# Heads 27 to 31 laid out so that neighbours in the ring come with one load

## The chip, the cores and the metric

The kernel runs on one core of a Trainium2 chip. A time is the device time in microseconds (us) of one execution of the whole program. The kernel before was run three times; its time is the median of these runs. All data is float32.

## The reference

Two layers, each an attention block against a cached K and V and a ReLU MLP, are applied twice over with the same weights and the same cache, to one token x of width 640:

```python
def _A_ref(x, k_cache, v_cache, wq, wo):          # 32 heads, 8192 keys, head width 128
    q = (x @ wq).reshape(1, 1, 32, 128).transpose(0, 2, 1, 3)
    scores = einsum("bhqd,bhkd->bhqk", q, k_cache) * (128 ** -0.5)
    p = softmax(scores, axis=-1)
    o = einsum("bhqk,bhkd->bhqd", p, v_cache)
    return o.transpose(0, 2, 1, 3).reshape(1, 1, 4096) @ wo

def _B_ref(x, w1, w2):                            # 640 -> 1728 -> 640
    return maximum(x @ w1, 0) @ w2

x = x + _A_ref(_layernorm(x), k_cache, v_cache, wq, wo)
x = x + _B_ref(_layernorm(x), w1, w2)
x = x + _A_ref(_layernorm(x), k_cache, v_cache, wq, wo)
x = x + _B_ref(_layernorm(x), w1, w2)
```

K and V of all heads are 256 MiB together, and both layers need all of it.

## The kernel before, in words

**The ring.** K and V come from DRAM into one SBUF tile, `ring`, of 8 x 4760 elements on each of 128 partitions. Places in it are counted in units of 8 elements. One head is 2048 units (16384 elements, 64 KiB on each partition): four K pieces and four V pieces of 256 units each. The whole ring thus holds a little more than two heads. Layer 0 goes through the heads 0 to 31, layer 1 through 31 to 0, so that what is in the ring at the change of layers can be used again: parts of heads 29 and 30 and all of 31, 3960 units (`KEPT`), stay there. The rest of the ring at that time (800 units) takes the blocks of w2, in four loads.

**Units of loading.** `UNITS` (L42) gives for each head the units in which it lies in DRAM. Heads 0 to 26 are one unit each, K and V together; `PARTS` (L44) says at which pieces the load of such a unit is cut. Heads 27 to 31 are cut into several units: 27 into K and V, 28 into four halves, 29 into ten units, 30 into five and 31 into six. `DROPPED` (L64) says from which unit on a head of 29 or 30 is kept for layer 1. Each unit is its own contiguous block in DRAM, with one row for each partition. The DRAM array is filled by `_laid_out` (L1006) on the host, in the order of `UNITS`.

**The order of the loads.** `todo` is a list of loads for the whole program, in order. An entry is a unit, the first and last piece, and a place in the ring or none. `pump` (L207) takes entries from its front as long as there is room: for an entry without a place `place` (L181) looks for a free stretch of the ring, and for the kept units of heads 29 and 30 `apart` (L123) gives the stretch to look in. If the entry at the front finds no room, `pump` stops; entries behind it don't overtake. `release` (L239) is called where the program has recorded the last matmul that reads a piece; it marks the piece's place free and calls `pump`. So each load stands on SyncE's queue behind the release that made room for it, and waits there for that matmul. A few loads go through ScalarE's queue instead: wq and wo of four heads at a time (tile `pair`), w1 and a rest of w2.

**The work of one head.** `scores` (L480) multiplies one K piece with the query, in eight matmul records, on TensorE; `row_maxima` and `exponentials` make the softmax with VectorE and ScalarE; `values` (L528) multiplies one V piece with the weights, again eight records; `output` (L562) sums four groups of rows. On TensorE the order is: scores of a head, softmax, values, output, scores of the next head. Only for the first three heads of layer 1 (`AHEAD`) do the next head's scores begin earlier. The lines that the profile names are L485 (scores), L534 and L552 (values), L456 (products with wo and w2), L667 (first MLP product) and L390 (`keep_busy`: matmuls without use that keep TensorE active, among them one in the softmax of the third last and of the second last head of a layer, and two between the second and third value piece of the second last head of layer 1).

**The end of a layer.** The second last head (30 in layer 0, 1 in layer 1) is projected through wo before the last head is done. `before_last` (L726) makes the layer norm and most of the first MLP product from that, between the scores of the last head (31, or 0). When the last head's values are there, a product with `mix` adds its share to the MLP, the hidden row is transposed, and the w2 blocks are multiplied, block by block. In layer 0 the release of the first two w2 blocks makes room for the fourth w2 load. After it SyncE loads units 0 and 1 of head 30 into two tiles that are no longer needed (`wct` and `mix`, `load_beside`, L227), and after that the first units of head 29 for layer 1, as the w2 blocks are done.

In layer 0 the loads from head 27 on stand in the order of heads and units: 27 K, 27 V, 28 in four, 29 in ten, 30 in five, 31 in six, w2 in four. In layer 1 they are: 29 in nine (the tenth is kept), 28 in four, 27 in two, 26 in two, and so on down to head 1 in four loads (`PARTS[1, 1]` = [2, 4, 6, 8], two pieces each), head 0 in six and w2 in four.

Of the kernel before, what the change touches and what calls it, by code (L numbers as in the profile page):

```python
# [43 lines left out]
PARTS = {(0, 0): [4, 9], (1, 26): [4, 8], (1, 25): [4, 8], (1, 2): [4, 8], (1, 1): [2, 4, 6, 8], (1, 0): [2, 4, 6, 7, 8, 9]}  # L44
# [19 lines left out]
DROPPED = {29: 9, 30: 2}  # L64
KEPT = 3960
# [40 lines left out]
def decode_kernel(ctx: ExitStack, tc: tile.TileContext, x, kv, wqo, w1, w2, w2_rest, out):  # L106
# [16 lines left out]
    apart = {(29, 9): (3800, KEPT), (30, 0): (4464, 4544), (30, 1): (4544, RING), (30, 2): (3072, 3800)}  # L123
# [3 lines left out]
    def all_of(layer, u):  # L127
        todo.append((layer, u, 0, len(UNITS[u[0]][u[1]][1]), None))
# [8 lines left out]
    def turning(layer, heads, slot):  # L137

        for h in heads:
            for a, end in parts_of(layer, h):  # L140
                while a < end:
                    b = min(end, a + SLOTS - slot)
                    todo.append((layer, (h, 0), a, b, SLOT * slot))
                    slot = (slot + b - a) % SLOTS
                    a = b

    def anywhere(layer, h):
        for a, b in parts_of(layer, h):
            todo.append((layer, (h, 0), a, b, None))
# [4 lines left out]
    for h in range(FULL[-1] + 1, H):  # L154
        for i in range(len(UNITS[h])):
            all_of(0, (h, i))
    for u in W2_ALL:
        all_of(0, u)
    for h in range(H)[:FULL[-1]:-1]:
        if h != 30:  # L160
            for i in range(len(UNITS[h])):
                if (h, i) not in kept:
                    all_of(1, (h, i))
# [5 lines left out]
    for u in W2_ALL:  # L169
        all_of(1, u)  # L170
    source = {}
    for us, dram in ((order, kv), (W2_ALL, w2)):
        o = 0
        for u in us:
            n = 8 * P * size(UNITS[u[0]][u[1]])
            source[u] = dram[o : o + n].rearrange("(p m) -> p m", p=P)
            o += n
# [29 lines left out]
    def pump():  # L207
        while todo:
            layer, u, first, last, at = todo[0]
            unit = UNITS[u[0]][u[1]]  # L210
            ns = [wide(kind_of(unit, t), piece) for t, piece in enumerate(unit[1])]
            n = sum(ns[first:last])
            if at is None:
                at = place(layer, u, n)
# [5 lines left out]
            o = 8 * sum(ns[:first])  # L220
            nc.sync.dma_start(ring[:, 8 * at : 8 * (at + n)], source[u][:, o : o + 8 * n])
            for t in range(first, last):
                live[layer, u, t] = at, ns[t]
                at_of[layer, u, t] = ring, 8 * at
                at += ns[t]

    def load_beside(where, at, n):  # L227
# [3 lines left out]
        nc.sync.dma_start(where[:, at : at + n], source[u])  # L231
# [774 lines left out]
def _laid_out(A_x, A_k_cache, A_v_cache, A_wq, A_wo, B_w1, B_w2):  # L1006
# [5 lines left out]
    for h in range(H):  # L1012
# [57 lines left out]
```

## Time and profile before

| | |
|---|---|
| median of 3 runs | 1349.7 us (1349.62 to 1351.87) |
| span of the profiled execution, first to last instruction | 1347.3 us |
| mean granted TensorE clock | 0.812 |
| TensorE busy with matmuls | 801.4 us |
| VectorE busy | 251.6 us |
| bytes moved by DMA | 574.55 MB, 426 GB/s over the span |
| share of SyncE's queue in the time of the 16 DMA engines | 91.7% |
| share of ScalarE's queue | 7.7% |
| loads | 157 |

The profiled execution is one of its own and not one of the three timed runs; what is known of its time is the span, which is 2.4 us below the median of the runs.

How to read it: a page of the profile gives busy time by engine, then the span in 40 slices, the DMA queues, the chain of work that ended last, the costliest groups of instructions and the DMA issues by size. Beside it the trace answers queries. A row of the timeline has start, duration, engine, line of the kernel, operation, output and inputs, shape and count; in square brackets stands how long the engine was idle before it and what ended that. A row of the chain has start, duration and what was done; for a DMA the duration is from its issue to its landing. A row of the windows has for one stretch of time each engine's busy time and number of instructions, then the granted TensorE clock (1 is full speed), the DMA engines' busy share and GB/s. A DMA share a little over 1 comes from packets that overlap.

### The profile page before, as it was taken

The page shows a single profiled execution, that of the slowest core. Times are in us where ns is not written, and L with a number is a line of the kernel's source. Part 1 is how long each engine was busy: PE and PEld are TensorE (multiplying, and loading weights), DVE is VectorE, ACT ScalarE, POOL GpSimd, SP SyncE. Part 2 cuts the span into 40 slices and gives each one's busy share as a digit, 9 for nine tenths or more (in the row PEclk, how much of TensorE's full clock was granted, in tenths as well). Part 3 has the DMA queues.
Part 4 walks back from the last instruction along what each step waited for, and adds up shares of the span by engine and source line. Part 5 has one row for each costly group of instructions (what it writes and reads, how often), then busy time and mean ns, then how long its engine had stood idle before and what let it go on. Part 6 is the DMA issues. An engine that isn't in the chain of part 4 may idle for free.

```text
span 1347.3 us, 13949 instructions
## 1 busy us (share of the span) xinstructions
PE 801.4 (59%) x6258; PEld 274.7 (20%) x6258; DVE 251.6 (19%) x798; ACT 58.5 (4%) x149; POOL 2.9 (0%) x10
## 2 busy tenths in 40 slices
PE   3455565563655655467688554456466554647777
PEld 1111111121211211122253111112122111212224
DVE  1121111221212211121223211122111121111222
ACT  0000000000000000000000000000000000000000
POOL 0000000000000000000000000000000000000000
PEclk9687677887978967787799877798778788877789
DMA  9999999999999999999999999999999999999997
GB/s 409 433 427 435 432 439 426 442 412 435 438 431 430 428 435 425 442 424 405 425 397 425 434 431 440 421 446 424 438 430 427 428 438 438 435 413 442 425 423 331
DMA packets 22675, 574.55 MB, mean 426 GB/s; under 512 B 2516, under 2 KB 2648, under 8 KB 5464
## 3 DMA queue, kind: packets, MB, share of 16 engines
q1 hardware_dynamic: 19592, 529.84, 91.7%
q10 hardware_dynamic: 3024, 43.83, 7.7%
q8 instruction: 49, 0.80, 0.2%
q14 instruction: 10, 0.08, 0.0%
HBM read 573.65 MB, written 0.00 MB: 426 GB/s over the span
## 4 chain that ended last, share of the span: by engine, by line
DMA 62%; PE 28%; DVE 6%; ACT 1%; issue 1%; another core or an unknown queue 1%; SPq 0%; ACTq 0%; DVEq 0%
DMA ring<-in_kv 61%; PE ps L485 14%; PE outs L534 9%; DVE h_t L496 2%; ACT p L510 1%; DMA pair<-in_wqo 1%; DVE pt L514 1%; PE pm L501 1%; DVE p L571 1%; PE px L424 1%; PE px L456 1%; PE acc L456 1%; DVE pT L516 0%; PE px L652 0%
## 5 line engine op out<-in xcount | busy, mean ns | idle before, releaser
L485 PE MATMUL ps<-ring,spread_q 128*32 128x512 f32 (+3 forms) x2104 | 328.4, 775 | 309.0 <-DMA ring<-in_kv 304.1
L534 PE MATMUL outs<-ring,pT 128*4 128x512 f32 (+1 forms) x2032 | 265.0, 665 | 41.5 <-DMA ring<-in_kv 24.7
L485 PEld LDWEIGHTS ps<-ring,spread_q 128*32 128x32 f32 x2104 | 77.6, 138 | 496.3 <-issue 296.9
L496 DVE TENSOR_REDUCE h_t<-ps 128x1 f32<-128x512 f32 x64 | 44.3, 692 | 612.5 <-PE ps L485 612.5
L510 ACT ACTIVATE p<-ps,h_t 128x512 f32<-128x512 f32 x64 | 44.0, 687 | 1225.5 <-DVE h_t L508 1225.5
L534 PEld LDWEIGHTS outs<-ring,pT 128*4 128x4 f32 x2032 | 51.2, 93 | 194.7 <-issue 169.9
L581 PE MATMUL pm<-ones,p 128*128 128x1 f32 x120 | 23.0, 260 | 94.9 <-DVE p L571 94.9
L567 DVE TENSOR_SCALAR p<-outs,ind 128x128 f32<-128x128 f32 x60 | 21.1, 351 | 262.1 <-PE outs L534 262.1
L571 DVE SCALAR_TENSOR_TENSOR p<-outs,ind,p 128x128 f32<-128x128 f32 x180 | 63.1, 351 | 6.4
L514 DVE STREAM_TRANSPOSE pt<-p 128x512 f32<-128x512 f32 x64 | 46.5, 727 | 58.5 <-ACT p L510 58.5
L501 PE MATMUL pm<-row_of,h_t 128*128 128x16 f32 x128 | 25.5, 274 | 49.9 <-DVE h_t L496 49.0
L581 PEld LDWEIGHTS pm<-ones,p 128*128 128x128 f32 x120 | 17.8, 188 | 151.7 <-DVE p L571 150.4
L501 PEld LDWEIGHTS pm<-row_of,h_t 128*128 128x128 f32 x128 | 19.2, 189 | 109.3 <-DVE h_t L496 107.4
L424 PE MATMUL px<-pair,ln_xc 128*32 128x256 f32 x280 | 34.6, 395 | 4.4 <-ACT mix L660 4.4
L652 PE MATMUL px<-w_t,wct 128*128 128x448 f32 (+1 forms) x80 | 35.1, 553 | 1.1 <-ACT wct L645 1.1
L523 PE MATMUL pm<-ind,h_t 128*128 128x1 f32 x128 | 23.6, 253 | 18.3 <-ACT p L510 18.3
L523 PEld LDWEIGHTS pm<-ind,h_t 128*128 128x128 f32 x128 | 22.1, 202 | 36.2 <-ACT p L510 27.2
L456 PE MATMUL acc<-pair,o_cols 128*32 128x160 f32 x496 | 21.6, 313 | 0.6 <-DVE o_cols L606 0.6
L424 PEld LDWEIGHTS px<-pair,ln_xc 128*32 128x32 f32 x280 | 15.6, 112 | 21.2 <-ACT mix L660 8.5
L582 DVE TENSOR_SCALAR o_cols<-pm,h_t 128x1 f32<-128x1 f32 x60 | 13.1, 218 | 30.3 <-PE pm L581 30.3
L508 DVE TENSOR_REDUCE h_t<-pm 128x1 f32<-128x16 f32 x64 | 11.2, 175 | 32.2 <-PE pm L501 32.2
L456 PEld LDWEIGHTS acc<-pair,o_cols 128*32 128x32 f32 x496 | 15.2, 113 | 3.9 <-issue 1.8
(119 smaller groups left out, 217.8 us busy)
## 6 DMA issues: line engine op xcount, KB each, us to landing
ring<-in_kv SPq DMA_DIRECT2D x24, 4096.0 KB, 30.5
ring<-in_kv SPq DMA_DIRECT2D x11, 6144.0 KB, 34.7
ring<-in_kv SPq DMA_DIRECT2D x31, 2048.0 KB, 31.1
pair<-in_wqo ACTq DMA_DIRECT2D x13, 2560.0 KB, 25.9
ring<-in_kv SPq DMA_DIRECT2D x14, 1024.0 KB, 12.7
ring<-in_w SPq DMA_DIRECT2D x4, 1280.0 KB, 25.8
w_t<-in_w ACTq DMA_DIRECT2D x1, 4320.0 KB, 27.7
pair<-in_wqo ACTq DMA_DIRECT2D x3, 1280.0 KB, 13.7
```

What stands on the lines that cost most here:

```text
L424: nc.tensor.matmul(pq[32 * j : 32 * j + 32, :n], xc[:, c : c + 1].to_broadcast([P, 32]), wq_t[g][:, c, j * n : (j + 1) * n], start=(c == 0 ...
L456: nc.tensor.matmul(acc[32 * g : 32 * g + 32, :DR], col.to_broadcast([col.shape[0], 32]), wt[:, g * DR : (g + 1) * DR], start=first, stop=last,
L485: nc.tensor.matmul(hd.ps[32 * g : 32 * g + 32, c : c + n], spread_q[:, 3 - r : 35 - r], tile_of[:, at + g * n : at + (g + 1) * n], start=f ...
L496: nc.vector.tensor_reduce(hd.nm, hd.ps, AX.X, ALU.max, negate=True)
L501: nc.tensor.matmul(pt[:, :16], hd.nm.to_broadcast([P, P]), row_of.rearrange("p g r -> p (g r)"), start=True, stop=True,)
L510: nc.scalar.activation(hd.p, hd.ps, AF.Exp, bias=hd.low, scale=1.0, accum_out=hd.l)
L514: nc.vector.transpose(pt, hd.p)
L523: nc.tensor.matmul(pt[:, :1], hd.l.to_broadcast([P, P]), ind[:, 4:5], start=True, stop=True)
L534: nc.tensor.matmul(hd.out[32 * g : 32 * g + 4, r : r + m].rearrange("p r d -> p (r d)"), hd.pT[:, 4 * i : 4 * i + 4], tile_of[:, v : v + m ...
L571: nc.vector.scalar_tensor_tensor(oc[:, r], hd.out[:, r], ind[:, r : r + 1], oc[:, r - 1], op0=ALU.mult, op1=ALU.add,)
L581: nc.tensor.matmul(pt[:, :1], oc[:, 3], ones, start=True, stop=True)
L652: nc.tensor.matmul(pt[:, :n], wct[:, c], w1_t[:, c, f : f + n], start=(c == 0), stop=(c == NB - 1),)
```

## The change

The loads around the change of layers are written out by hand. `ROWS` says which units lie side by side in DRAM: each of the heads 0 to 28 is a row, the units of heads 29 and 30 together are one row in a new order, and head 31 is a row. `ENDS` lists the loads from head 27 on in layer 0, `STARTS` the first loads of layer 1 down to head 27. One load can now take several units that are neighbours in the row and in the ring. The kept units of 30 and 29 come earlier in layer 0: unit 2 of head 30 with unit 9 of head 29 between the K and the V of head 28, and units 0 and 1 of head 30 after that V, ahead of head 29's other units. In `PARTS` head 1 of layer 1 has two loads of four pieces and no longer four of two. `pump` and `_laid_out` follow. In layer 0 there are 12 loads fewer, in layer 1 six.

```diff
-PARTS = {(0, 0): [4, 9], (1, 26): [4, 8], (1, 25): [4, 8], (1, 2): [4, 8], (1, 1): [2, 4, 6, 8], (1, 0): [2, 4, 6, 7, 8, 9]}
+PARTS = {(0, 0): [4, 9], (1, 26): [4, 8], (1, 25): [4, 8], (1, 2): [4, 8], (1, 1): [4, 8], (1, 0): [2, 4, 6, 7, 8, 9]}
...
+ROWS = [[(h, i) for i in range(len(UNITS[h]))] for h in range(29)]
+ROWS.append([(29, i) for i in (0, 1, 2, 3, 6, 4, 5, 7, 8)] + [(30, 2), (29, 9), (30, 0), (30, 1), (30, 3), (30, 4)])
+ROWS.append([(31, i) for i in range(len(UNITS[31]))])
+ENDS = [
+    [(27, 0), (27, 1)],
+    [(28, 0), (28, 1)],
+    [(30, 2), (29, 9)],
+    [(28, 2), (28, 3)],
+    [(30, 0), (30, 1)],
+    ROWS[29][:5],
+    ROWS[29][5:9],
+    [(30, 3)],
+    [(30, 4)],
+] + [[u] for u in ROWS[30]]
+STARTS = [
+    [(29, 0)],
+    [(29, 1)],
+    [(29, 2)],
+    [(29, 3)],
+    ROWS[29][4:8],
+    [(29, 8)],
+    [(28, 0), (28, 1)],
+    [(28, 2)],
+    [(28, 3)],
+    [(27, 0)],
+    [(27, 1)],
+]
...
-    apart = {(29, 9): (3800, KEPT), (30, 0): (4464, 4544), (30, 1): (4544, RING), (30, 2): (3072, 3800)}
+    apart = {(30, 2): (3072, KEPT), (30, 0): (4464, RING)}
...
-    for h in range(FULL[-1] + 1, H):
-        for i in range(len(UNITS[h])):
-            all_of(0, (h, i))
-    for u in W2_ALL:
-        all_of(0, u)
-    for h in range(H)[:FULL[-1]:-1]:
-        if h != 30:
-            for i in range(len(UNITS[h])):
-                if (h, i) not in kept:
-                    all_of(1, (h, i))
+    for us in ENDS + [[u] for u in W2_ALL]:
+        all_of(0, us)
+    for us in STARTS:
+        all_of(1, us)
...
-            nc.sync.dma_start(ring[:, 8 * at : 8 * (at + n)], source[u][:, o : o + 8 * n])
-            for t in range(first, last):
-                live[layer, u, t] = at, ns[t]
+            u, t = pieces[0]
+            block, o = source[u]
+            unit = UNITS[u[0]][u[1]]
+            o += 8 * sum(wide(kind_of(unit, i), unit[1][i]) for i in range(t))
+            nc.sync.dma_start(ring[:, 8 * at : 8 * (at + n)], block[:, o : o + 8 * n])
+            for (u, t), m in zip(pieces, ns):
+                live[layer, u, t] = at, m
                 at_of[layer, u, t] = ring, 8 * at
-                at += ns[t]
+                at += m
```

The orders of TensorE, VectorE, ScalarE and GpSimd are the same instructions in the same order before and after; only the line numbers differ (L520 and L569 take the places of L485 and L534). What moves stands on SyncE's queue. The numbers in its rows are partitions and elements on each partition; 4096 elements are a 2048 KB load.

On SyncE in layer 0, from the last of the undivided heads to the loads of head 30, before: the rows are two undivided loads, the second of them head 26 (16384), then 27 (8192), 28 (4096), 29 (from 2048 to 1280), the kept units 0 and 1 of 30 (640, 1728), and behind these rows 30's unit 2 (5824), its V and head 31.

```order
L221 DMA ring<-in_kv 128x16384 x2
L221 DMA ring<-in_kv 128x8192 x2
L221 DMA ring<-in_kv 128x4096 x4
L221 DMA ring<-in_kv 128x2048 x2
L221 DMA ring<-in_kv 128x1024
L221 DMA ring<-in_kv 128x1280
L221 DMA ring<-in_kv 128x2048 x2
L221 DMA ring<-in_kv 128x512
L221 DMA ring<-in_kv 128x2048 x2
L221 DMA ring<-in_kv 128x1280
L221 DMA ring<-in_kv 128x640
L221 DMA ring<-in_kv 128x1728
```

And the same place after: the third 16384 is head 27, 8192 is head 28's K, 7104 the kept units 2 of head 30 and 9 of head 29, 8192 head 28's V, 2368 the kept units 0 and 1 of head 30, 6912 head 29's K and 8192 its V.

```order
L255 DMA ring<-in_kv 128x16384 x3
L255 DMA ring<-in_kv 128x8192
L255 DMA ring<-in_kv 128x7104
L255 DMA ring<-in_kv 128x8192
L255 DMA ring<-in_kv 128x2368
L255 DMA ring<-in_kv 128x6912
L255 DMA ring<-in_kv 128x8192
L255 DMA ring<-in_kv 128x4096 x5
```

The kept units moved from behind head 29 to ahead of it, so that between head 29's V and the K halves of head 31 (the third and fourth of the five 4096 rows) only two loads are left.

On SyncE at the end of layer 1, before: heads 3 and 2 (8192), then head 1 in four loads and the first three of head 0 (4096), and the rest of head 0.

```order
L221 DMA ring<-in_kv 128x8192 x4
L221 DMA ring<-in_kv 128x4096 x7
L221 DMA ring<-in_kv 128x2048
L221 DMA ring<-in_kv 128x1024 x2
L221 DMA ring<-in_w 128x2560 x2
```

And after, where head 1 stands among the 8192 rows:

```order
L255 DMA ring<-in_kv 128x8192 x6
L255 DMA ring<-in_kv 128x4096 x3
L255 DMA ring<-in_kv 128x2048
L255 DMA ring<-in_kv 128x1024 x2
L255 DMA ring<-in_w 128x2560 x2
```

Four loads of 4096 became two of 8192: head 1's K and its V each land as a whole.

59 lines of the change are left out of this document (35 added, 24 removed).

## The prediction

> **What bounds the kernel now.** First the page of the profile, its head, its second and its third part.
>
> ```profile
> span 1347.3 us, 13949 instructions
> ...
> PE 801.4 (59%) x6258; PEld 274.7 (20%) x6258; DVE 251.6 (19%) x798; ACT 58.5 (4%) x149; POOL 2.9 (0%) x10
> ...
> DMA  9999999999999999999999999999999999999997
> ...
> DMA packets 22675, 574.55 MB, mean 426 GB/s; under 512 B 2516, under 2 KB 2648, under 8 KB 5464
> ```
>
> The DMA engines are busy in every fortieth of the span but the last. So whatever moves the time either makes the stream of loads shorter, stops it, or acts after its last load. The table of DMA issues says how far ahead the stream is issued: half of the 2048 KB loads land 31.1 us or more after their issue.
>
> ```profile
> ring<-in_kv SPq DMA_DIRECT2D x11, 6144.0 KB, 34.7
> ring<-in_kv SPq DMA_DIRECT2D x31, 2048.0 KB, 31.1
> ```
>
> Next the windows: two stretches with large rows and with rows of 8 KB, and three around the change of layers (time, then PE, PEld, DVE, ACT, POOL; the last three numbers are the granted clock, the DMA share and GB/s).
>
> ```profile
> 646.00:650.00 4.00, 0.51 (x20) 0.24 (x12) 0.00 (x0) 0.00 (x0) 0.00 (x0) 0.92 1.01 416
> 820.00:860.00 40.00, 20.16 (x170) 6.09 (x170) 5.55 (x17) 1.56 (x4) 0.00 (x0) 0.79 1.00 432
> 630.00:640.00 10.00, 7.13 (x48) 1.73 (x40) 2.15 (x7) 0.78 (x2) 0.00 (x0) 0.83 0.93 372
> 690.00:700.00 10.00, 9.18 (x196) 6.79 (x184) 2.59 (x14) 0.61 (x3) 0.00 (x0) 1.00 0.93 366
> 700.00:710.00 10.00, 8.63 (x132) 5.07 (x126) 2.19 (x13) 0.00 (x0) 1.10 (x2) 1.00 1.00 396
> ```
>
> There is little to win: 16 GB/s where rows are small, 1.4 us of stream at 630 to 640 ((432 - 372) x 10 / 432), and 2.4 us at 690 to 710 (66 and 36 GB/s below 432, for 10 us each).
>
> Last the chain that ended last, around the change of layers and at the end.
>
> ```profile
> 658.73 22.56 DMA ring<-in_kv
> ...
> 681.34 1.97 PE ps L485 x16
> ...
> 1294.64 28.89 DMA ring<-in_kv
> ...
> 1323.57 1.97 PE ps L485 x16
> ...
> 1342.90 1.27 PE px L456 x32
> ```
>
> And from SyncE's timeline the issue of the last w2 load of layer 0, and of the first eight ring loads of layer 1.
>
> ```profile
> 696.78 0.33 SPq L221 DMA_DIRECT2D ring<-in_w  x1
> ...
> 699.75 11.31 SPq L221 DMA_DIRECT2D ring<-in_kv  x8
> ```
>
> In both layers the second K half of the last head lands (658.73 + 22.56 = 681.29; 1294.64 + 28.89 = 1323.53), TensorE scores it at once, and from there the chain is compute only: in layer 0 to the release that lets SyncE issue the last w2 load at 696.78, which restarts a stream that had run dry, and in layer 1 to the end. The stream and TensorE therefore meet at two points. A gain of the stream counts only if TensorE is ready there, and lateness of TensorE counts in full, because the ring is full of kept heads and nothing else can be loaded.
>
> **How ready TensorE is.** The timeline of TensorE before the first point: the last scores of head 29 (its last K piece), its values, scores of 30, its values, first K piece of 31, the last MLP step, second K half of 31.
>
> ```profile
> 651.91 1.29 PE L485 MATMUL ps<-ring,spread_q 128*32 128x320 f32 x8 [5.40 <-DMA ring<-in_kv]
> ...
> 656.78 4.99 PE L534 MATMUL outs<-ring,pT 128*4 128x512 f32 x32
> ...
> 664.46 3.49 PE L485 MATMUL ps<-ring,spread_q 128*32 128x80 f32 x40
> ...
> 671.31 3.62 PE L534 MATMUL outs<-ring,pT 128*4 128x512 f32 x32 [0.64 <-DVE pT L516]
> ...
> 677.20 1.04 PE L485 MATMUL ps<-ring,spread_q 128*32 128x512 f32 x8
> ...
> 680.29 0.50 PE L667 MATMUL px<-w_t,ln_xc 128*32 128x192 f32 x8
> ...
> 681.34 1.93 PE L485 MATMUL ps<-ring,spread_q 128*32 128x512 f32 x16 [0.56 <-DMA ring<-in_kv]
> ```
>
> TensorE has 0.56 us to spare. And before the second point, in layer 1: scores of head 1, its four value pieces with fillers (L390) between the pairs, the projection, the two K halves of head 0.
>
> ```profile
> 1301.63 1.06 PE L485 MATMUL ps<-ring,spread_q 128*32 128x512 f32 x8
> ...
> 1303.06 2.88 PE L485 MATMUL ps<-ring,spread_q 128*32 128x512 f32 x24
> ...
> 1309.30 1.90 PE L534 MATMUL outs<-ring,pT 128*4 128x512 f32 x16 [0.64 <-DVE pT L516]
> ...
> 1311.13 2.31 PE L390 MATMUL px<-w_t 128*128 128x512 f32 x4
> ...
> 1313.79 1.90 PE L534 MATMUL outs<-ring,pT 128*4 128x512 f32 x16 [0.35 <-DMA ring<-in_kv]
> ...
> 1317.66 0.48 PE L456 MATMUL acc<-pair,o_cols 128*32 128x160 f32 x8 [0.31 <-DVE o_cols L606]
> ...
> 1318.69 1.06 PE L485 MATMUL ps<-ring,spread_q 128*32 128x512 f32 x8 [0.55 <-DMA ring<-in_kv]
> ...
> 1321.80 0.49 PE L667 MATMUL px<-w_t,ln_xc 128*32 128x192 f32 x8
> ...
> 1323.57 1.92 PE L485 MATMUL ps<-ring,spread_q 128*32 128x512 f32 x16 [1.28 <-DMA ring<-in_kv]
> ```
>
> Here it has 0.35, 0.55 and 1.28 us to spare, one after the other. The waits at 1313.79, 1318.69 and 1323.57 are 4.9 us apart: that is what one 2048 KB load takes.
>
> **Part one: 18 loads fewer.** A 1024 KB load (1.049 MB) takes 2.52 us at 416 GB/s and 2.43 at 432, so each load that goes saves at most some 0.09 us, and no less than nothing; most merged rows are shorter than those at 820, so I take 0.075. 12 go before 681 and 6 in layer 1: 0.9 + 0.45 = 1.35 us at the stream's own end. As a check, from head 27's first load to 681.29 the loads are 38144 KB (39.1 MB, with the wo load on ScalarE's queue), which at 432 GB/s take 90.4 us, against the 91.6 us from the end of this wait:
>
> ```profile
> 589.75 6.10 PE L485 MATMUL ps<-ring,spread_q 128*32 128x512 f32 x32 [5.62 <-DMA ring<-in_kv]
> ```
>
> So 1.2 us is all that this stretch can give, the dent at 630 to 640 included: the loads that TensorE waits for lose next to nothing there. I take 0.9 for the stretch, with 0 and 1.2 as ends.
>
> **Part two: larger loads are issued later.** Head 27's load waits for the sixth piece of head 25 and not the second, later by half its scores, a softmax and two value pieces: some 9 us by the rows above (half of 6.10, 3.6, half of 4.99). With 31 us between issue and landing this costs nothing, and up to 9 us if that lead were gone. The shortest lead is after the restart: pieces 4 to 7 of head 29 go out together where the last of the eight issues from 699.75 stood, just before 711. Ahead of them stand 1024, 1024, 512, 640 and (ScalarE) 1280 KB, 10.7 us of stream that begins at 699.75 at the earliest and behind wct's and mix's 1184 KB (2.8 us). So the queue lasts to 710.5 or, more likely, 713. I take zero; 2.5 us (three pieces of scores) at worst.
>
> **Part three: kept pieces ahead of head 29.** SyncE now loads the 7104 and 2368 elements a partition that stay for layer 1 (4.85 MB, 11 us) before head 29's K and V. After head 29's V come only four 2048 KB loads up to the second K half of 31, that one among them: it lands at 681.29 - 4 x 4.9 - 0.9 = 660.8. Its values stood at 656.78 before. K lands one V load (twice 4.9 us) earlier, at 651.0; scoring all of it cold takes the 6.1 us of the row at 589.75, and 3.58 us lie between the last score and the first value (653.20 to 656.78): 660.8 as well. So the values start 4.0 us late; behind them on TensorE's queue stand heads 30 and 31 and the MLP, and SyncE waits for the releases of these. They took 4.99 us half throttled; the same 32 at full clock took 3.62 (row at 671.31). The clock rose just there:
>
> ```profile
> 650.00:660.00 10.00, 7.23 (x34) 2.40 (x38) 2.06 (x6) 0.78 (x2) 0.00 (x0) 0.52 1.03 434
> 660.00:670.00 10.00, 7.52 (x90) 2.67 (x78) 2.49 (x7) 0.54 (x1) 0.00 (x0) 1.00 1.01 427
> ```
>
> Starting at 660.8, after six unbroken microseconds of scores, I take 3.62: values end at 664.4 and not 661.8, 2.6 us late. All from there to 680.79 is compute in fixed order, without a wait for DMA. Less the 0.56 to spare: TensorE takes up 31's second K half 2.05 us later than before, at 683.4. If the values run cold it is 3.4.
>
> The Trainium skill, page "TensorE: Matmul & The Clock Gate", section "Part 1: The HAM clock gate", says that about 3.4 us of sustained matmuls release the throttle and that an idle window of that length brings it back. The trace's 0.52 and 1.00 fit; by it the value 3.62 holds, by the row at 656.78 it would be 4.99 and the whole sum 1.4 us more.
>
> The restart at 696.78 is 2.05 us later with it. The stream is not shifted by all of that, since some engines were still busy with earlier loads:
>
> ```profile
> 697.00:698.00 1.00, 1.00 (x36) 0.88 (x31) 0.21 (x2) 0.00 (x0) 0.00 (x0) 1.00 0.74 242
> 698.00:699.00 1.00, 1.00 (x25) 0.36 (x17) 0.33 (x2) 0.00 (x0) 0.00 (x0) 1.00 0.86 261
> ```
>
> At most 0.5 us can be made good so: the shift is 1.5 to 2.05, I take 1.8. What part one gained in layer 0 is lost here, as waiting.
>
> **Part four: head 1 in two loads at the end.** Its K lands whole where the second half landed, and its V whole at 1313.74. The values, 16 + four fillers + 16, took 1309.30 to 1315.69 less the 0.35 wait: 6.0 us, formerly with half of them before the last landing. Now they start at 1313.8. K, at about 1304 instead of 1301.63, is not the limit: 4.3 us of scores (1301.63 to 1305.94) and 3.36 to the first value (1309.30) end at 1311.7, and even cold at about 1313.7. So 1313.8 + 6.0 = 1319.8, + 2.45 to the end of the projection (1315.69 to 1318.14) = 1322.2, + 3.6 to the end of L667 (1318.69 to 1322.29) = 1325.8, against 1323.57: 2.25 us late, all three spare times used up. With the 0.45 us of layer 1's six loads: 1.8 us.
>
> **Sum.** 1347.3 + 1.8 + 1.8 = 1350.9 us of span; the chain behind is the same. The median of the runs, 1349.7, is 2.4 above the profiled span, so 1353.3 us, 0.27% slower. Parts by their ends: 1.5 to 3.4 and 1.3 to 3.3 (head 1's values cold, 1.4 more).
>
> **The rivals.**
>
> *TensorE catches up* (not slower). It needs 3.4 of the 4.0 us in layer 0 and nearly all at the end, through idle time that the rows do not show, above all if V of 29 lands before about 658.7. Then only the loads saved count: 1349.7 - 1.35 = 1348.35. For it: TensorE is busy for only 59% of the span. Against it: the two spare times are read at the very places. Chance 0.15.
>
> *Only one of the two points is late.* Layer 0 alone: 1349.7 + 1.8 - 0.45 = 1351.05; the end alone: 1349.7 - 0.9 + 1.8 = 1350.6. Chance 0.13.
>
> *Cold values at both points*: 1353.3 + 1.4 + 1.4 = 1356.1. For it: the 32 matmuls at 589.75 took 6.10 us, those at 656.78 4.99. Chance 0.08.
>
> *Slower reads.* Heads 29 and 30 now lie in one row of 32768 elements, so their loads read pieces 128 KiB apart. Loads that read pieces 64 KiB apart (the 6144 KB ones) run in the 432 GB/s window, so nothing is seen at half the distance; were they to read at 416, 25.7 MB would take 2.3 us more: 1355.6. Chance 0.05. The Trainium skill, page "DMA: Bandwidth & Descriptors", section "Latency and other measured facts", gives 207 GB/s at a pitch of 512 KiB where a padded one gave 214; an estimate by that page, at four times this pitch, is 2.0 us.
>
> *The stream gets seamless* at 690 to 710 too (faster): 1349.7 - 1.35 - 2.4 = 1345.95. Nothing in the change issues w2 earlier. Chance 0.04.
>
> That loads are not merged is excluded: SyncE's order shows 18 fewer, and the other engines' orders are equal.
>
> **How the numbers follow.** The forecast has 0.55, within 1352 to 1355. The range 1350.0 to 1356.5 takes in it, the one-point case, cold values and slow reads, 0.8 together; left out are TensorE that catches up and the seamless stream. A measurement of this kernel tells about 0.2% (2.7 us) from no change: slower is above 1352.4. Of the forecast 0.44 lies there, with cold and slow reads 0.13, and 0.02 of the rest: 0.59. Faster, below 1347.0, is the seamless stream, 0.04. Same is 0.37.
>
> **What would show it.** Right: head 29's values (L569 in the new numbering) wait for a DMA and start near 660.8; 31's second K half is taken up near 683.4 with no DMA wait; the last w2 load of layer 0 is issued near 698.8; head 1's first value waits for a DMA, and the last K half of head 0 does not; the dent at 630 to 640 is gone. Wrong: a DMA wait of TensorE still ahead of 31's second K half or of head 0's, or any fall of GB/s below 420 where heads 29 and 30 are read.

## The result, and the profile after

| | before | after |
|---|---|---|
| median of 5 runs | 1349.7 us (1349.27 to 1351.87) | 1357.93 us (1355.91 to 1359.65) |
| span of the profiled execution | 1347.3 us | 1355.7 us |
| time of the profiled execution | not known; some 1349.1 by the 1.8 us of the others | 1357.51 us, 1.8 above its span |

The ratio is 1.0056, with a 95% interval of 1.0045 to 1.0067: slower, as forecast, but by 8.2 us and not by 3.6, and above the top of the range (1356.5).

The page of the profile after, the lines that answer to those of before:

```profile
span 1355.7 us, 13914 instructions
...
PE 810.3 (60%) x6258; PEld 279.4 (21%) x6258; DVE 251.6 (19%) x798; ACT 58.5 (4%) x149; POOL 2.9 (0%) x10
...
DMA  9999999999999999999979999999999999999996
...
DMA packets 20083, 574.55 MB, mean 424 GB/s; under 512 B 2228, under 2 KB 2360, under 8 KB 4280
...
ring<-in_kv SPq DMA_DIRECT2D x11, 6144.0 KB, 36.6
ring<-in_kv SPq DMA_DIRECT2D x21, 2048.0 KB, 35.6
```

The same bytes come in 2592 packets fewer, and the DMA row has a 7 now, in the slice that begins at 678 us (21st of 40, 33.9 us each): the stream stands still at the change of layers. PE is busy for 8.9 us more with the same 6258 matmuls, so more of them ran at half clock in this execution. The sum alone says little: in a run of the kernel before with a few fillers more (before_held, below) PE is busy for 814.3 us, and the time is that of before.

TensorE's timeline of after at the first point, from the scores of head 29 to the second K half of head 31:

```profile
651.15 6.41 PE L520 MATMUL ps<-ring,spread_q 128*32 128x512 f32 x56 [4.72 <-DMA ring<-in_kv]
...
660.92 3.62 PE L569 MATMUL outs<-ring,pT 128*4 128x512 f32 x32 [0.64 <-DVE pT L551]
...
667.41 4.99 PE L520 MATMUL ps<-ring,spread_q 128*32 128x80 f32 x40
...
675.76 3.62 PE L569 MATMUL outs<-ring,pT 128*4 128x512 f32 x32 [0.64 <-DVE pT L551]
...
681.64 1.04 PE L520 MATMUL ps<-ring,spread_q 128*32 128x512 f32 x8
...
685.01 1.93 PE L520 MATMUL ps<-ring,spread_q 128*32 128x512 f32 x16
```

The first two rows are where the prediction put them (651.0 and 660.8, 3.62 long). The values wait for VectorE and not for the DMA: V had landed 0.18 us earlier (660.74 by its completion marks, the times at which the trace has the parts of a load done). The third row is not where it was put: head 30's scores took 4.99 us instead of 3.49. In the last row nothing stands in brackets: TensorE no longer waits for 31's second K half, which had landed at 680.29 by its completion marks, and takes it up at 685.01, 3.67 us later than before. The windows show why the row of those scores is long (time, PE busy; the last three numbers are granted clock, DMA share, GB/s):

```profile
663.60:667.00 3.40, 1.74 (x34) 0.71 (x27) 1.62 (x5) 0.00 (x0) 0.00 (x0) 1.00 1.03 439
667.00:670.40 3.40, 3.40 (x36) 1.45 (x35) 0.00 (x0) 0.00 (x0) 0.00 (x0) 0.50 1.02 429
690.00:700.00 10.00, 8.97 (x157) 6.06 (x161) 2.21 (x11) 0.74 (x3) 0.00 (x0) 1.00 0.49 204
697.00:701.00 4.00, 3.54 (x60) 2.52 (x64) 1.37 (x8) 0.37 (x2) 0.00 (x0) 1.00 0.04 14
700.00:710.00 10.00, 9.09 (x187) 6.49 (x179) 2.96 (x17) 0.00 (x0) 1.10 (x2) 1.00 0.81 286
630.00:640.00 10.00, 3.85 (x28) 1.14 (x24) 1.97 (x6) 0.78 (x2) 0.00 (x0) 0.81 0.97 413
```

The granted clock is 0.50 for 3.4 us; before, it was 1.00 from 660 on. The last four rows are the stream: the dent at 630 to 640 is nearly gone (413 GB/s, before 372), but 690 to 700 went from 366 to 204 and 700 to 710 from 396 to 286, and at 697 to 701 next to nothing moves. The last w2 load, which restarts it, is issued 3.69 us later than before, on SyncE's timeline:

```profile
700.47 0.33 SPq L255 DMA_DIRECT2D ring<-in_w  x1
```

And TensorE's timeline at the end of layer 1: scores of head 1, its first two V pieces, fillers, its last two, the K halves of head 0, and the last product:

```profile
1308.88 1.93 PE L520 MATMUL ps<-ring,spread_q 128*32 128x512 f32 x8 [0.95 <-DMA ring<-in_kv]
...
1311.62 3.02 PE L520 MATMUL ps<-ring,spread_q 128*32 128x512 f32 x24
...
1318.61 3.31 PE L569 MATMUL outs<-ring,pT 128*4 128x512 f32 x16 [1.24 <-DMA ring<-in_kv]
1321.84 2.55 PE L425 MATMUL px<-w_t 128*128 128x512 f32 x4
1324.33 1.90 PE L569 MATMUL outs<-ring,pT 128*4 128x512 f32 x16
...
1328.49 1.04 PE L520 MATMUL ps<-ring,spread_q 128*32 128x512 f32 x8
...
1331.87 1.93 PE L520 MATMUL ps<-ring,spread_q 128*32 128x512 f32 x16
...
1351.14 1.29 PE L491 MATMUL px<-ring,hT 128*32 128x160 f32 x32
```

The first values wait for the DMA, as predicted, and take 3.31 us for what took 1.90 before, again at half clock; both K halves of head 0 are taken up without a wait. The last landed at 1328.26 and waited 3.6 us for TensorE. So of the 8.3 us by which this row stands later than before (1331.87 - 1323.57), 4.7 are the stream, and 3.6 TensorE at the end.

### The profile page after: what moved, and what is told of

Same layout as the page of the kernel before. It is cut to its first block, busy times and chain, and to the rows that moved or that the text cites. A ratio compares the mean times of both kernels' runs of the same rounds, so it can differ in the third digit from the quotient of the medians.

```text
span 1355.7 us, 13914 instructions
## 1 busy us (share of the span) xinstructions
PE 810.3 (60%) x6258; PEld 279.4 (21%) x6258; DVE 251.6 (19%) x798; ACT 58.5 (4%) x149; POOL 2.9 (0%) x10
## 4 chain that ended last, share of the span: by engine, by line
DMA 63%; PE 28%; DVE 5%; ACT 1%; issue 1%; another core or an unknown queue 1%; ACTq 0%; SPq 0%; DVEq 0%
DMA ring<-in_kv 63%; PE ps L520 14%; PE outs L569 8%; DVE h_t L531 2%; DVE pt L549 1%; ACT p L545 1%; PE pm L536 1%; PE px L491 1%; DVE p L606 1%; PE px L459 1%; DVE pT L551 0%; PE acc L491 0%; DVE h_t L543 0%; PE pm L629 0%
## 5 line engine op out<-in xcount | busy, mean ns | idle before, releaser
L520 PE MATMUL ps<-ring,spread_q 128*32 128x512 f32 (+3 forms) x2104 | 333.8, 788 | 307.2 <-DMA ring<-in_kv 304.0
L569 PE MATMUL outs<-ring,pT 128*4 128x512 f32 (+1 forms) x2032 | 266.0, 668 | 42.7 <-DMA ring<-in_kv 25.9
L520 PEld LDWEIGHTS ps<-ring,spread_q 128*32 128x32 f32 x2104 | 80.4, 141 | 494.0 <-issue 311.8
L569 PEld LDWEIGHTS outs<-ring,pT 128*4 128x4 f32 x2032 | 51.2, 93 | 196.7 <-issue 174.8
```

Source lines behind the costliest of these rows:

```text
L520: nc.tensor.matmul(hd.ps[32 * g : 32 * g + 32, c : c + n], spread_q[:, 3 - r : 35 - r], tile_of[:, at + g * n : at + (g + 1) * n], start=f ...
L569: nc.tensor.matmul(hd.out[32 * g : 32 * g + 4, r : r + m].rearrange("p r d -> p (r d)"), hd.pT[:, 4 * i : 4 * i + 4], tile_of[:, v : v + m ...
```

## The experiments

The theory after this result: the kept pieces ahead of head 29 and head 1 in two loads make TensorE late at the two points, each by more than predicted because the clock falls there. The rival: the loads themselves, fewer and larger, disturb the stream, and the two places only show it. Twelve kernels were run. In the table, the ratio is to runs of the kernel before on the same chip, with its 95% interval; the last two columns are, in one profiled execution each, when TensorE takes up 31's second K half and when the last w2 load is issued. Line numbers in these kernels differ by a few.

| run | loads fewer | median us | ratio | 31's K | last w2 |
|---|---|---|---|---|---|
| before, profiled | 0 | 1349.7 | | 681.34 | 696.78 |
| after | 18 | 1357.93 | 1.0056 (1.0045, 1.0067) | 685.01 | 700.47 |
| kept_behind | 17 | 1353.19 | 1.0025 (1.0016, 1.0034) | 681.19 | 696.63 |
| head1_four | 16 | 1352.33 | 1.0023 (1.0012, 1.0033) | 686.67 | 702.12 |
| both_undone | 15 | 1352.42 | 1.0015 (1.0006, 1.0024) | 682.98 | 698.40 |
| before_head1_two | 2 | 1352.17 | 1.0016 (1.0007, 1.0025) | 681.29 | 696.73 |
| order_only | 0 | 1354.44 | 1.0031 (1.0019, 1.0043) | 685.24 | 700.70 |
| clock_held | 18 | 1354.63 | 1.0033 (1.0021, 1.0045) | 683.32 | 698.78 |
| split_27 | 14 | 1350.36 | 0.9998 (0.9989, 1.0006) | 680.44 | 695.88 |
| merge_less | 14 | 1349.69 | 0.9990 (0.9967, 1.0012) | 682.26 | 697.71 |
| held_starts_apart | 14 | 1355.80 | 1.0037 (1.0023, 1.0051) | 685.24 | 700.70 |
| before_held | 0 | 1350.38 | 1.0002 (0.9993, 1.0011) | 681.14 | 696.58 |
| less_held | 14 | 1349.07 | 0.9991 (0.9982, 1.0000) | 680.82 | 696.26 |
| less_held_27 | 13 | 1349.29 | 0.9994 (0.9985, 1.0003) | 680.91 | 696.36 |

The kernel before had a median of 1350.04 us beside the first four, 1350.22 beside order_only, clock_held, split_27 and merge_less, 1350.19 beside the next three and 1350.09 beside the last.

**The kept pieces behind head 29 again** (kept_behind).

```diff
-    [(30, 2), (29, 9)],
     [(28, 2), (28, 3)],
-    [(30, 0), (30, 1)],
     ROWS[29][:5],
     ROWS[29][5:9],
+    [(29, 9)],
+    [(30, 0), (30, 1)],
+    [(30, 2)],
...
-    apart = {(30, 2): (3072, KEPT), (30, 0): (4464, RING)}
+    apart = {(30, 2): (3072, 3800), (29, 9): (3800, KEPT), (30, 0): (4464, RING)}
```

> The changed kernel with the kept units of heads 30 and 29 loaded behind head 29's V again, as before; 17 loads fewer than before and not 18, head 1 still in two loads. Theory (TensorE is late at the two points where it meets the stream): head 29's values no longer wait, 31's second K half is taken up on landing, the 3.7 us of layer 0 go; the end stays about 3.6 us late: 1352.5 us (1351.5 to 1354). Rival (merged loads themselves, by a later issue or by rows 128 KiB apart, slow the stream): no gain from the order, 1357 us.

1353.19 us, as the theory said. In its timeline the first point is as before, with the wait for the DMA back, and the end is late as in after:

```profile
656.70 4.54 PE L570 MATMUL outs<-ring,pT 128*4 128x512 f32 x32
...
681.19 1.92 PE L521 MATMUL ps<-ring,spread_q 128*32 128x512 f32 x16 [0.94 <-DMA ring<-in_kv]
...
1314.28 3.41 PE L570 MATMUL outs<-ring,pT 128*4 128x512 f32 x16 [1.56 <-DMA ring<-in_kv]
...
1327.40 1.93 PE L521 MATMUL ps<-ring,spread_q 128*32 128x512 f32 x16
```

**Head 1 in four loads again** (head1_four): `(1, 1): [4, 8]` back to `(1, 1): [2, 4, 6, 8]`.

> The changed kernel with head 1 of layer 1 in four loads again. Theory: the last K half of head 0 is taken up on landing, 3.6 us of lateness at the end go, two loads cost 0.15 us: 1354.4 us (1353.5 to 1355.5), and the change of layers looks as in the changed kernel. Rival (merged loads slow the stream): 1357.5 us, since two small merges make no difference.

1352.33 us, below what the theory gave (1353.5 at least), far below the rival. The profiled execution is the slowest of the eight, 1355.76; in it TensorE is late at the first point (686.67), with head 29's values and head 30's scores both slow:

```profile
660.88 5.31 PE L569 MATMUL outs<-ring,pT 128*4 128x512 f32 x32 [1.52 <-DMA ring<-in_kv]
...
669.19 4.86 PE L520 MATMUL ps<-ring,spread_q 128*32 128x80 f32 x40
```

At the end the theory holds in it: the last K half of head 0 landed at 1329.96 and was taken up at 1330.20, 0.24 us later and not 3.6.

**Both undone** (both_undone): the two diffs together.

> Both of the above undone, 15 loads fewer than before: only merging is left of the change. Theory: TensorE meets the stream on time at both points and the stream is 15 x 0.075 = 1.1 us shorter: 1348.6 us (1347.6 to 1350.2). Rival (merged loads slow the stream): as slow as what the order does not explain, 1353 us or more.

1352.42: neither. With both of the theory's causes gone the kernel should have been a little faster than before, and it is 0.15% slower, so merging the loads costs something of its own. The windows of this kernel show where the stream falls short:

```profile
614.00:618.00 4.00, 2.59 (x18) 0.62 (x10) 0.87 (x2) 0.28 (x1) 0.00 (x0) 0.89 0.71 262
626.00:629.00 3.00, 1.42 (x10) 0.58 (x14) 1.62 (x5) 0.00 (x0) 0.00 (x0) 0.92 0.92 350
```

The stream, at 426 and 411 GB/s there before, lacks there (426 - 262) x 4 / 426 + (411 - 350) x 3 / 411 = 2.0 us. Head 27, now one load, lands whole at 609.09, so its scores begin late, their releases come late, and the load of head 28's V is issued at 616.27, when nothing but the rest of 28's K is under way. In after the 7104 kept elements stood ahead of that V and filled the gap (402 GB/s at 614 to 618).

What the hole costs is not fixed. kept_behind is the same program up to head 1 of layer 1, and its windows have the hole too:

```profile
614.00:618.00 4.00, 2.06 (x18) 0.58 (x10) 0.87 (x2) 0.78 (x2) 0.00 (x0) 0.97 0.79 287
...
626.00:629.00 3.00, 3.00 (x48) 1.22 (x40) 0.00 (x0) 0.00 (x0) 0.00 (x0) 1.00 0.86 371
```

Yet 31's second K half landed at 681.14 there, as before, and in both_undone at 682.92. Between 618 and 640 the clock stayed at 1.00 in kept_behind, and head 27's values took 3.62 us; in both_undone they took 6.34, and the releases behind them came later.

**Head 1 in two loads in the kernel before** (before_head1_two): `(1, 1): [2, 4, 6, 8]` to `(1, 1): [4, 8]` in the kernel before, nothing else.

> The kernel before with one edit: head 1 of layer 1 in two loads. Theory: 2.3 us late at the end if TensorE's clock holds, 3.6 if its values begin at half clock, less 0.15 for two loads: 1352.9 us (1351.7 to 1353.6). Rival (size of loads alone counts): 1349.6 us.

1352.17, as the theory said. The first point is as before, and the end is late (the first scores of head 1, its first values, the last K half of head 0):

```profile
1305.84 1.94 PE L485 MATMUL ps<-ring,spread_q 128*32 128x512 f32 x8 [1.74 <-DMA ring<-in_kv]
...
1315.98 1.90 PE L534 MATMUL outs<-ring,pT 128*4 128x512 f32 x16 [0.64 <-DVE pT L516]
...
1327.59 1.93 PE L485 MATMUL ps<-ring,spread_q 128*32 128x512 f32 x16
```

Here it is K that came late for TensorE, with scores at half clock (1.94 us for what took 1.06); the values wait for VectorE. The last K half of head 0 landed at 1325.20 and waited 2.39 us for TensorE, near the 2.25 of the prediction.

**The order alone in the kernel before** (order_only): no load merged, head 1 in four.

```diff
-    for h in range(FULL[-1] + 1, H):
-        for i in range(len(UNITS[h])):
-            all_of(0, (h, i))
+    early = [(27, 0), (27, 1), (28, 0), (28, 1), (30, 2), (29, 9), (28, 2), (28, 3), (30, 0), (30, 1)]
+    for u in early + [u for u in order if u[0] > FULL[-1] and u not in early]:
+        all_of(0, u)
```

> The kernel before, no load merged, with the kept units early: 30's unit 2 and 29's unit 9 behind 28's K halves, 30's units 0 and 1 behind 28's V halves, ahead of head 29. Theory: the order alone makes TensorE late at the first point; nothing is gained by fewer loads, so head 29's last V piece lands near 661.8, TensorE takes up 31's second K half 3 to 4.5 us late, and the time is 1349.9 + 3 to 4.5 = 1353.6 (1352.5 to 1355). Rival: it takes the merging to make the order cost (a head in units of 2048 KB and less lets TensorE score and multiply while the rest lands): 1350.5 at most.

1354.44, as the theory said. The order alone makes TensorE 3.9 us late at the first point, and at the end of layer 1 it waits for the DMA again, 4.56 us later than before, so nothing of the lateness of the restart was made good:

```profile
656.83 1.72 PE L485 MATMUL ps<-ring,spread_q 128*32 128x128 f32 x16 [4.33 <-DMA ring<-in_kv]
...
662.13 4.31 PE L534 MATMUL outs<-ring,pT 128*4 128x512 f32 x32
...
685.24 1.93 PE L485 MATMUL ps<-ring,spread_q 128*32 128x512 f32 x16
...
1328.13 1.92 PE L485 MATMUL ps<-ring,spread_q 128*32 128x512 f32 x16 [1.28 <-DMA ring<-in_kv]
```

**The clock held** (clock_held): the changed kernel with three groups of matmuls without use more, one in each layer ahead of the last product of the output of the third last head, one ahead of head 1's values.

```diff
                 next(steps)
+                if where == H - 3:
+                    keep_busy(1)
...
+            if L and near_end:
+                keep_busy(1)
```

> The changed kernel with one group of matmuls without use more ahead of the last product of head 29's (layer 1: head 2's) output, and one ahead of head 1's values. Nothing else differs. Theory: of TensorE's 3.7 and 3.6 us of lateness, 1.5 and 1.3 are the granted clock, which fell to 0.50 for 3.4 us at just these places in the changed kernel's trace; with TensorE kept active it stays at 1.00 there, and the time falls from 1357.9 by up to 2.8, to 1355.2 (1354 to 1356.5). Rival: the clock is not held by this, or the waits eat what it gives: 1357.9 (within 0.7).

1354.63, as the theory said; by the ratios 0.0023 less than after, 3.1 us, with an uncertainty of some 2. In its profiled execution the clock stayed at 1.00 from 656 to 706, and the first point came out as the prediction had worked it out for full clock (683.4 and 698.8):

```profile
660.92 3.62 PE L569 MATMUL outs<-ring,pT 128*4 128x512 f32 x32 [1.21 <-DMA ring<-in_kv]
...
667.21 3.49 PE L520 MATMUL ps<-ring,spread_q 128*32 128x80 f32 x40
...
683.32 1.93 PE L520 MATMUL ps<-ring,spread_q 128*32 128x512 f32 x16
```

The same execution lost time elsewhere (its own was 1357.46). Its clock was at half from 707 to 716, and the load of four pieces of head 29 that the change made for layer 1 was issued at 717.83, behind scores that took 6.36 us. The windows:

```profile
717.00:720.00 3.00, 2.07 (x22) 0.53 (x18) 0.77 (x2) 0.00 (x0) 0.00 (x0) 1.00 0.61 181
...
706.00:716.00 10.00, 9.36 (x74) 4.86 (x78) 1.40 (x8) 0.00 (x0) 0.55 (x1) 0.54 1.01 414
```

181 GB/s for 3 us is 1.7 us of stream lost at 426. At the end head 1's first values took 1.90 us and not 3.31, but TensorE is still late there, as head 1 is still in two loads.

**Head 27 in two loads** (split_27): both_undone with `[(27, 0)], [(27, 1)]` for `[(27, 0), (27, 1)]`. It has 14 loads fewer than before; the expectation miscounts them.

> The run with both parts undone, and head 27 again in two loads, K and V (11 loads fewer than before, kept units behind head 29, head 1 in four). Theory: the hole in the stream at 614 to 618 and the second at 627 came from head 27 landing whole, so that its scores begin late and the releases for 28's V and 29's K come late; with K of head 27 landing first both holes go, TensorE takes up 31's second K half on time, and the time is 1349.4 (1348.6 to 1350.5). Rival: the hole comes from merging 28's or 29's loads: 1352.4 as with both parts undone.

1350.36, inside the theory's range: the 2 us of both_undone are gone. 614 to 618 has 393 GB/s, and 626 to 629 has 424. But 14 loads fewer are worth nothing here either: TensorE and the restart are 0.9 us earlier, and head 29's first load of layer 1, issued at 698.85 and not 699.75, lands at 707.47 and not 707.14. What held it up there the trace doesn't show.

**Less merging** (merge_less): the changed kernel with head 1 in four loads and this in `ENDS` (14 loads fewer, not 13):

```diff
     [(28, 2), (28, 3)],
+    ROWS[29][:2],
+    ROWS[29][2:5],
+    ROWS[29][5:7],
+    ROWS[29][7:9],
     [(30, 0), (30, 1)],
-    ROWS[29][:5],
-    ROWS[29][5:9],
```

> The changed kernel with head 1 in four loads, head 29 in four loads (K in two, V in two) ahead of 30's units 0 and 1, and only 30's unit 2 with 29's unit 9 (7104 elements) early as cover: 13 loads fewer than before. Theory: head 29's V lands 2.5 us earlier than in the changed kernel and half of its values are done before, the cover keeps the stream full at 614 to 618, so TensorE takes up 31's second K half at most 0.7 us late, and the time is 1349.3 (1348.4 to 1350.6). Rival: any early kept load makes TensorE late by its 8 us of stream: 1352 or more.

1349.69, the theory's time, though TensorE is 0.9 us late at the first point and not at most 0.7: half of head 29's values are done before its last V lands, and then the clock falls twice, during the other half (3.57 us and not 1.90) and during head 30's scores:

```profile
658.19 3.57 PE L571 MATMUL outs<-ring,pT 128*4 128x512 f32 x16 [2.60 <-DMA ring<-in_kv]
...
664.45 5.18 PE L522 MATMUL ps<-ring,spread_q 128*32 128x80 f32 x40
```

**Less merging and the clock held** (less_held): merge_less with clock_held's first insertion.

> The run with less merging (14 loads fewer than before: head 29 in four loads ahead of 30's units 0 and 1, head 1 in four), with one group of matmuls without use ahead of the last product of head 29's output. Theory: in the run without it TensorE took up 31's second K half 0.9 us late only because the clock fell to 0.50 during head 30's scores (5.18 and not 3.49 us); with the clock held it is on time (near 680.6), the stream keeps what 14 loads save before the first point, up to 1 us, and the time is 1349.0 (1348.2 to 1349.9), some 0.7 under that run. Rival: what the loads save ends as idle DMA time ahead of the restart whatever TensorE does: 1349.9, no better than before.

```profile
658.08 1.90 PE L571 MATMUL outs<-ring,pT 128*4 128x512 f32 x16 [1.05 <-DMA ring<-in_kv]
...
662.65 3.49 PE L522 MATMUL ps<-ring,spread_q 128*32 128x80 f32 x40
...
680.82 1.92 PE L522 MATMUL ps<-ring,spread_q 128*32 128x512 f32 x16 [1.29 <-DMA ring<-in_kv]
```

At the first point TensorE waits for the DMA again, with 1.29 us to spare. The median is 1349.07, 1.1 us below the kernel before; the interval reaches 1.0000, so this is at the edge of what can be told, and by its ratio it is not better than merge_less (its runs spread less, up to 1351.3 against 1354.0).

**The same in the kernel before** (before_held): clock_held's first insertion alone.

> The kernel before with the same group of matmuls without use ahead of the last product of head 29's (layer 1: head 2's) output; nothing merged or moved. Theory: the kernel before waits for the DMA at both points and loses nothing to the clock there, so nothing changes: 1350.0 (1349.4 to 1350.6). Rival: a fall of the clock costs the kernel before time too, and holding it is worth something by itself: 1349.2 or less.

1350.38: nothing changes, as the theory said. In its execution head 29's values still took 4.96 us, and TensorE waited 0.58 us for the DMA at the first point, as before. At the end head 1's first values ran at half clock (3.52 us), and the last K half of head 0 was still taken up on landing (1324.81 and 1324.85): there the time to spare took up one such fall.

**Layer 1's first loads apart** (held_starts_apart): clock_held with `ROWS[29][4:8]` as four loads and `[(28, 0), (28, 1)]` as two.

> The run with the clock held, and layer 1's first loads apart again: head 29's units 4 to 7 in four loads and 28's K in two (14 fewer than before in all). Theory: in the run with the clock held the load of four pieces was issued at 717.83, behind scores at half clock, and the DMA engines were idle for about 2 us at 717 to 720; with the pieces issued one by one that goes, and the time falls by up to 1.5 us in the executions that have it: 1353.6 (1352.8 to 1354.6). Rival: the late issue costs nothing on the whole: 1354.6, as with the clock held alone.

1355.8, a miss for the theory; the rival's 1354.6 is within the uncertainty. In the profiled execution the share at 717 to 720 is full (410 GB/s), but the filler did not hold the clock: it fell one step later, during head 30's values, for about the same price. Up to the first loads of layer 1 this is clock_held's program, so the same filler holds the clock in one execution and not in another.

```profile
667.47 3.49 PE L524 MATMUL ps<-ring,spread_q 128*32 128x80 f32 x40
...
674.32 5.27 PE L573 MATMUL outs<-ring,pT 128*4 128x512 f32 x32 [0.64 <-DVE pT L555]
...
685.24 1.93 PE L524 MATMUL ps<-ring,spread_q 128*32 128x512 f32 x16
```

**Less merging, the clock held, head 27 in two loads** (less_held_27).

> The run with less merging and the clock held, and head 27 in two loads again (13 loads fewer than before). Theory: with head 27 whole its scores begin late and 28's V is issued late, which costs that run part of what it saves before the first point, although the kept load covers most of it; TensorE had 1.3 us to spare there, so with head 27 in two loads the time falls by 0.3 to 0.9, to 1348.5 (1348.0 to 1348.9). Rival: the cover already hides it and nothing changes: 1349.1 (1348.9 to 1349.6).

1349.29, the rival's case: with the kept load as cover, head 27 in one load costs nothing.

## Why the prediction was right in the sign and wrong in the size

**Part one (fewer loads).** 0.9 us was expected at the stream's end in layer 0. The four profiled executions with these 12 loads fewer in the new order (after, head1_four, clock_held, held_starts_apart) land 31's second K half at 680.29 to 680.38, the four with none fewer there (before, before_held, before_head1_two, order_only) at 681.09 to 681.33: 0.7 to 1.0 us, so the term holds. (In its check, 681.29 less 589.75 is 91.5 and not 91.6.) Whether the 0.45 us of layer 1 came can't be told: in after the landing of head 0's last K half is 4.7 us late, 1.0 more than the 3.69 us of the restart, but from the restart to that landing the executions of before, before_held, before_head1_two and order_only take between 626.8 and 628.5 us, and after 627.8.

**Part two (larger loads later).** The zero is right for the changed kernel in layer 0, but the reason given, 31 us between issue and landing, is not. both_undone has that lead in the median too (33.1) and is slower than before, and split_27 shows that head 27 in one load does it. What counts, as far as less_held and less_held_27 show, is that something else is queued behind that load; in after it is the kept pieces. In layer 1 clock_held's execution lost 1.7 us of stream to the load of four pieces, inside the bound of 2.5, but held_starts_apart without that load was no faster, so no cost on the whole is shown.

**Part three (kept pieces first).** The order, the landing of head 29's V (660.74 by the marks, worked out as 660.8), its values (3.62 us) and the price at full clock (683.32 in clock_held, worked out as 683.4) are right, and order_only shows that the order alone costs 0.31%. The step that failed is "All from there to 680.79 is compute in fixed order, without a wait for DMA": the steps were taken at the durations of before, and one of them, head 30's scores, took 1.50 us more at half clock. The prediction asked whether the values run cold, and not whether anything behind them does. Of "At most 0.5 us can be made good so" nothing showed: in order_only the lateness was 3.9 at the restart and 4.56 at the end, and in after the DMA engines had run dry by the restart (14 GB/s at 697 to 701). The 0.25 us that the sum took from it is less than executions differ by.

The rival of slow reads is out: were 29's rows 128 KiB apart read slower, its V could not have landed as worked out. From 641 to 661, when head 29 is read in after, the stream ran at 426 GB/s, and at 425 in before, whose rows are shorter; the 10 us windows in it lie on both sides of the 420 that the prediction named as a sign (435 and 418). The Trainium skill, page "DMA: Bandwidth & Descriptors", section "Latency and other measured facts", gives a loss at a pitch of 512 KiB, for copies between HBM tensors; at 128 KiB no run here shows one.

**Part four (head 1 in two loads).** The wait is the one predicted, and before_head1_two shows the cost by itself, 0.16%, 2.1 us. In after it was 3.6 us instead of 2.25, since the first values ran at half clock: 3.31 - 1.90 = 1.4, the amount that the prediction had put down for cold values and left out of its forecast. That K "is not the limit" failed in before_head1_two: there its scores at half clock, and not V, set when the values began.

**The sum.** Predicted for the first point and layer 1 were 1.35 us (1.8 less 0.45), found 4.7; for the end 2.25 and 3.6. Of the 3.35 us between 1.35 and 4.7, 1.6 are the lateness beyond 2.05, mostly clock, 0.25 the part that was not made good, and 1.5 the gain of layer 1 and the 1.0 us of part one. That last piece has no cause that a run shows. Part of it can be the profiled execution of before, whose span of 1347.3 is shorter than that of every one of the 88 runs of this kernel beside the experiments (1347.7 at the least). The case of "cold values at both points", 1356.1, had the right mechanism with a chance of 0.08; in layer 0 one of the steps from head 29's values on ran at half clock, in part at least, in every profiled execution with a late TensorE but clock_held's. (In before these values did too, 4.99 us, but there they began early enough.) By the ratios the order (0.31%) and head 1 (0.16%), each alone in the kernel before, make 0.47% of the 0.56%; the rest is within the intervals. They do not simply add: undone in the changed kernel, the order is worth 0.31%, head 1 0.33% and both 0.41%, each to within some 0.15%; and 0.15% is left, which is head 27 in one load without the kept pieces as cover.

## What to carry to other kernels

Where stream and compute meet at one point, read how much idle time the compute engine has there before loads are reordered: a load that is needed later must not stand ahead of one whose user has only half a microsecond to spare. It can stand there when the loads behind it are cut so that work begins on a part: merge_less and less_held keep 7104 of these elements early, with head 29 in four loads, and lose nothing that can be measured. A merged load saved under 0.1 us here, and it delays both the first use and the release by the rest of the load, so merge only where something else is queued to cover that, as in less_held_27. When a step is moved, take the durations behind it at both clocks, not at the one that the profile happens to show.

## What the runs showed of the hardware

**The clock.** In the 3.4 us ahead of the fall in after TensorE was busy for 1.74 us (the windows above), and the clock then fell to 0.50 for 3.4 us. The longest gap there is this one, on TensorE's timeline of after:

```profile
666.20 0.38 PE L616 MATMUL pm<-ones,p 128*128 128x1 f32 x2 [1.66 <-DVE p L606]
```

The same step of the kernel before has the same gap, and the clock stayed at 1.00:

```profile
663.44 0.38 PE L581 MATMUL pm<-ones,p 128*128 128x1 f32 x2 [1.67 <-DVE p L571]
```

The gap alone thus does not decide. In all of these traces the granted clock changes on a grid of 3.41 us, which lies differently in each execution (in after the changes are at 656.77, 667.01 and 670.43, in before at 649.36 and 659.60). In after the gap lies within one cell of the grid; in before it is shared by two, in which TensorE was busy for 2.17 and 2.99 us. The six falls that the traces have between 655 and 684 (in after, head1_four, merge_less and held_starts_apart) all follow a cell in which TensorE was busy for 1.82 us or less, and no cell at full clock there with 2.0 us or more is followed by one. Two cells with 1.75 us, in both_undone and split_27, kept the clock, and elsewhere some falls follow busier cells, so a threshold is not shown.

Where the fall comes, and whether it does, changes from execution to execution: after and head1_four are one program up to head 1 of layer 1, and head 29's values took 3.62 us in the one and 5.31 in the other. That this makes part of the spread of after's runs (3.7 us from lowest to highest) is likely and not shown, since one run of each kernel was profiled. The Trainium skill, page "TensorE: Matmul & The Clock Gate", section "Part 1: The HAM clock gate", calls the window free-running and 3.4 us long, with which the trace agrees. The same section of the Trainium skill gives an idle window as what throttles; in the 3.4 us ahead of this fall TensorE worked for half of the time.

**Sixteen engines out of step.** A load has 16 completion marks in the trace, read here as one for the share of each DMA engine; a wait of TensorE ends with the last (681.29 and 681.34 in before). By the marks of 31's second K half, the first engine was done 2.3 us before the last in the kernel before (678.97 and 681.29), and 5.2 us before it in after (675.05 and 680.29). In before the distance is 8.1 us for a load that lands at 639.47, and 2.4 for the one that lands at 645.31, behind the dent at 630 to 640. So in the dent, it seems, the engines that were ahead had nothing queued, and the others caught up. order_only fills it (418 GB/s), and there the first engine has 31's second K half at 676.08 and the last at 681.33. The new order moved the first engine by 2.9 us and the landing by nothing. Here, then, the dent in the mean DMA share was no gain to be had, since the slowest engine had no part in it.
